# Last chunk's gelu from PSUM on ScalarE, and the last spatial pass over one token tile with its sums evacuated, added and gated

## The chip, the cores and the metric

The kernel runs on one core of one Trainium2 chip. The metric is device microseconds of one execution; lower is better. "Before" is the kernel as it was, "after" the changed one.

Engine names are those of the profile: PE is TensorE, ACT is ScalarE, DVE is VectorE, POOL is GpSimd. L12 is line 12 of the kernel that the line belongs to, so the same work has another line number in another kernel.

## The reference

Two layers, each a multi-query attention (32 heads of 16, one shared key and value head, 2048 tokens, 512 features) and a gated mixer. All inputs are bf16. Only the mixer is changed:

```python
def _B_ref(x, w_in, w_sp, b_sp, w_out):          # x [1, 2048, 512]
    z = _gelu(x @ w_in)                           # tanh form, F = 1792
    z1 = z[..., :Fh]                              # Fh = 896
    z2 = _layernorm(z[..., Fh:], axis=-1)
    g = einsum('ts,bsf->btf', w_sp, z2) + b_sp    # mixes TOKENS: [2048 x 2048]
    return (z1 * g) @ w_out

x = x + _A_ref(_layernorm(x), ...)                # layer 0
x = x + _B_ref(_layernorm(x), ...)
x = x + _A_ref(_layernorm(x), ...)                # layer 1
x = x + _B_ref(_layernorm(x), ...)
```

The product with `w_sp` needs z2 of all tokens before any output token is finished. So the end of each mixer is a serial stretch: the last tokens leave attention, pass through gelu and the norm, and only then can the last part of the sum over tokens be done. (einsum with `@` is shortened here.)

## The kernel before

The program is emitted by a small list scheduler of its own. Each operation has an engine (sometimes two to choose from), an assumed duration and a priority, and the scheduler decides the order on every engine.

The mixer works through token chunks, and the spatial product is taken in passes over token tiles of 128. Three passes run while attention still runs and leave their sums in `gp` (fp16, in SBUF); the last pass is over tiles 14 and 15:

```python
self.chunks = [512, 512, 512, 256, 128, 128]
self.passes = [(0, 8, 1), (8, 12, 2), (12, 14, 3)]   # (first tile, end, after chunk)
self.s_fin = 14                                       # last pass: tiles 14, 15
PR_SMALL = 1.0                                        # priority of the small chunks
```

The gelu of each chunk comes after its copies out of PSUM. Both z2 and z1 are copied, then both gelus run in SBUF, and the statistics of z2 wait for both:

```python
ge = sc.op("act", gl, ..., z1 + z2, -1.0, table="gelu")      # gl: gelu of z1, then of z2
...
s_ = [sc.op("dve", <bn_stats of one half of z2>, 0.53, [ge], ...) for h in range(2)]
```

The last pass adds the earlier sums inside PSUM, by a product with the identity; DVE then gates straight from PSUM (for each of 8 groups of 256 tokens):

```python
if final:
    todo.append(("g", None))                 # ident16 x gp: adds the earlier sums
todo += [("w", w) for w in ws]               # z2 x w_sp, one matmul per token tile
...
pl, (ev,) = sc.job(pieces, [dict(            # hT = PSUM * z1, 512 columns each
    fn=lambda e, b, ...: e.tensor_tensor(self.hT[:, par, f0:f0 + m, :], <PSUM>, z1r[...], ALU.mult), ...)])
```

After it come 14 matmuls of 512 columns with `w_out` for each 256 tokens, and DVE adds the residual.

The softmax here doesn't subtract the row's maximum and nothing guards it: scores larger than these inputs give would overflow.

## Time and profile before

| | before |
|---|---|
| median time, first measurement (3 runs) | 1933.82 us (1931.3 to 1937.45) |
| span of the profiled execution, mean granted clock | 1933.2 us, 0.977 |
| layer 0: last exp of attention ends / layer 1: first exp starts | 905.2 / 955.6 us |
| layer 0: last residual add, about / layer 1: first exp on DVE | 997 / 1005.5 us |
| layer 1: last exp ends, and from there to the end ("tail") | 1861.9 us, 71.3 us |

The exps of the softmax bound most of the span, so two numbers divide it well: the tail, and the time from layer 0's last exp to layer 1's last exp ("last to last", 956.7 us), which holds layer 0's transition and layer 1's attention.

Busy time by engine, from the page of before:

```profile
PE 1649.2 (85%) x17431; PEld 671.0 (35%) x17431; DVE 1777.4 (92%) x3198; ACT 1747.3 (90%) x1526; POOL 59.7 (3%) x106
```

PE, DVE and ACT are all busy on average. But the average mixes stages. The table of windows of before shows the stretch after layer 0's last exp. Its columns are: the window, its length, then busy time (and instructions) of PE, PE weight loads, DVE, ACT and POOL, then the granted clock, the share of DMA and GB/s:

```profile
925.00:945.00 20.00, 17.85 (x111) 11.95 (x112) 14.37 (x28) 0.00 (x0) 1.73 (x4) 0.83 0.18 51
945.00:965.00 20.00, 19.64 (x162) 11.61 (x160) 15.23 (x35) 11.43 (x15) 2.82 (x6) 1.00 0.27 71
...
985.00:1005.00 20.00, 17.57 (x133) 8.70 (x130) 11.85 (x23) 11.41 (x14) 1.87 (x4) 1.00 0.00 1
```

ACT, which is 90% busy over the span, has no work from 925 to 945, and the granted clock of PE is 0.83 there. The same view for the tail of layer 1:

```profile
1862.00:1882.00 20.00, 19.30 (x205) 15.42 (x203) 17.15 (x35) 6.44 (x9) 0.77 (x2) 1.00 0.34 97
1882.00:1902.00 20.00, 18.74 (x131) 12.53 (x132) 16.35 (x31) 0.00 (x0) 0.78 (x2) 1.00 0.30 90
1902.00:1922.00 20.00, 20.00 (x135) 13.01 (x133) 13.76 (x25) 0.00 (x0) 0.00 (x0) 1.00 0.45 134
```

Here PE is busy for 58 of 60 us, and ACT has nothing after 1882. PE is the limit, and the work that PE has left is the length of the tail.

The timeline of ACT at layer 1's last chunk (columns: start, duration, engine, line, operation, times; in brackets the idle time before and who ended it):

```profile
1848.69 13.24 ACT L1257 ACTIVATE Pa<-ps_all 128x1024 bf16<-128x1024 f32 x12
...
1874.53 0.54 ACT L887 ACTIVATE z2n<-ps_all 128x448 bf16<-128x448 f32 x1 [1.57 <-PE ps_all L876]
...
1876.18 1.16 ACT L913 ACTIVATE E<-ps_all 128x512 bf16<-128x512 f32 x2 [0.35 <-PE ps_all L902]
1877.36 1.28 ACT L921 ACT_TABLE_LOAD   x1
1878.66 0.95 ACT L921 ACTIVATE E<-E 128x896 bf16<-128x896 bf16 x1
1879.51 0.93 ACT L922 ACTIVATE z2n<-z2n 128x896 bf16<-128x896 bf16 x1
```

The last exps end at 1848.69 + 13.24 = 1861.93. The four copies end at 1877.34, the table load at 1878.64, both gelus at 1880.44. DVE then takes the statistics and, after a small POOL step, the normalisation:

```profile
1880.84 1.14 DVE L934 BATCH_NORM_STATS2 st_18<-z2n 128x6 f32<-128x448 bf16 x2
...
1884.09 0.51 DVE L943 TENSOR_SCALAR z2n<-z2n,mv_19,rs_21 128x896 bf16<-128x896 bf16 x1
```

So z2 is ready at 1884.60, and PE starts the last pass at 1885.25, as the timeline of PE shows:

```profile
1885.25 0.28 PE L1032 MATMUL ps_all<-gp,ident_3 128*128 128x256 f16 x1 [0.63 <-DVE gp L1050]
...
1889.30 3.19 PE L1087 MATMUL ps_all<-E 128*128 128x512 bf16 x14
```

The first line is an identity matmul. Small matmuls here have a pitch of 0.108 us, `w_out` matmuls 0.216 us (3.19 us for 14, of which the last 0.17 is drain). In layer 0 the same chain left PE idle, and then slow:

```profile
919.56 3.44 PE L1034 MATMUL ps_all<-wsT,z2n 128*128 128x256 bf16 x30
927.15 0.40 PE L1032 MATMUL ps_all<-gp,ident_3 128*128 128x256 f16 x1 [4.15 <-DVE z2n L943]
927.34 0.63 PE L1034 MATMUL ps_all<-z2n 128*128 128x256 bf16 x2
```

4.15 us idle; and the second pair of lines shows a pitch of about 0.2 us where it was 3.44 / 30 = 0.115 before the gap. The Trainium skill, "TensorE: Matmul & The Clock Gate", section Why this matters for your kernels, says that PE-idle gaps of more than about 3 us drop the matmul rate to half. This trace agrees: after 4.15 us, half pace for about 4.6 us.

The groups by form of the tail of before (busy time and mean ns of one after the first bar, idle time before them after the second):

```profile
L1032 PE MATMUL ps_all<-gp,ident_3 128*128 128x256 f16 x56 | 15.3, 273 | 0.6 <-DVE gp L1050 0.6
...
L1061 DVE TENSOR_TENSOR E<-ps_all,z1s 128x512 bf16<-128x512 f32 x24 | 15.6, 684 | 0.0
```

56 identity matmuls; and DVE's gate from PSUM takes 684 ns for 512 columns.

### The profile page before, as it was taken

How to read it: one execution, taken by the hardware profiler on the slowest of the kernel's cores; microseconds unless marked ns; L12 is line 12 of the kernel's file. 1: busy time of each engine (PE TensorE's matmuls, PEld its weight loads, DVE VectorE, ACT ScalarE, POOL GpSimd, SP SyncE). 2: the span in 40 equal slices, each digit the busy share in tenths (PEclk: the TensorE clock that was granted, in tenths of full speed). 3: DMA queues.
4: the chain of work that ended last, by engine and by line, in shares of the span. 5: the costliest groups of instructions: out<-in, count | busy, mean ns of one | idle time of the engine just before them, and what ended most of it. 6: DMA issues, size and time to landing. Idle time of an engine off the chain costs nothing.

```text
span 1933.2 us, 41389 instructions
## 1 busy us (share of the span) xinstructions
PE 1649.2 (85%) x17431; PEld 671.0 (35%) x17431; DVE 1777.4 (92%) x3198; ACT 1747.3 (90%) x1526; POOL 59.7 (3%) x106
## 2 busy tenths in 40 slices
PE   6777887787989998889987877877788999888899
PEld 3222222122234443555542222222122444335565
DVE  7999999999998898987769999989999899999976
ACT  7999999999999999997379999999999999999960
POOL 3000000000000000000000000000000000000000
PEclk9999999999999999999999999999998999989999
DMA  9700001000001000112100000010000100010123
GB/s 262 191 1 1 1 1 42 1 1 1 1 31 34 23 8 26 46 28 62 53 10 1 1 1 1 1 42 1 1 1 20 34 23 23 2 53 8 29 71 101
DMA packets 96985, 59.84 MB, mean 31 GB/s; under 512 B 39704, under 2 KB 92704, under 8 KB 96800
## 3 DMA queue, kind: packets, MB, share of 16 engines
q1 hardware_dynamic: 95216, 56.64, 10.6%
q8 instruction: 138, 2.26, 0.5%
q10 hardware_dynamic: 1584, 0.56, 0.1%
q14 instruction: 47, 0.39, 0.1%
HBM read 30.97 MB, written 17.83 MB: 25 GB/s over the span
## 4 chain that ended last, share of the span: by engine, by line
ACT 32%; PE 30%; DVE 25%; issue 12%; POOL 1%; ACTq 0%; POOLq 0%
ACT Pa L1257 29%; PE ps_all L1034 8%; PE ps_all L1540 7%; DVE E L1437 5%; PE ps_all L1333 4%; DVE Pd L1475 4%; PE ps_all L1087 3%; DVE E L1473 2%; DVE E L1464 2%; DVE E L1470 2%; DVE gp L1050 2%; PE ps_all L1523 1%; PE ps_all L748 1%; DVE E L1467 1%; ACT z2n L922 1%
## 5 line engine op out<-in xcount | busy, mean ns | idle before, releaser
L1257 ACT ACTIVATE Pa<-ps_all 128x1536 bf16<-128x1536 f32 (+1 forms) x1435 | 1640.0, 1349 | 59.6 <-PE ps_all L1540 46.0
L1540 PE MATMUL ps_all<-qs,kT 32*128 32x512 bf16 (+2 forms) x6144 | 572.8, 315 | 227.9 <-ACT Pa L1257 213.9
L1540 PEld LDWEIGHTS ps_all<-qs,kT 32*128 32x128 bf16 x6144 | 172.6, 92 | 710.1 <-ACT Pa L1257 631.0
L1437 DVE TENSOR_SCALAR E<-ps_all 128x512 int32<-128x512 f32 x510 | 347.9, 685 | 26.8 <-PE ps_all L1540 24.0
L1333 PE MATMUL ps_all<-Pa,V 128*32 128x512 bf16 (+2 forms) x5407 | 331.4, 316 | 2.0 <-DVE oT L771 1.5
L1475 DVE SCALAR_TENSOR_TENSOR Pd<-E 128x1024 uint16<-128x1024 int32 x255 | 310.2, 1217 | 0.8
L1523 PE MATMUL ps_all<-wo_r,zero 128*128 128x512 bf16 (+2 forms) x967 | 257.2, 369 | 2.2 <-DVE E L1437 1.8
L1034 PE MATMUL ps_all<-wsT,z2n 128*128 128x256 bf16 x1456 | 216.8, 276 | 4.7 <-DVE gp L1050 2.9
L1333 PE MATMUL ps_all<-Pd,V 128*32 128x512 bf16 (+2 forms) x737 | 181.0, 324 | 0.0
L1470 DVE TENSOR_TENSOR E<-E 128x1024 f16<-128x1024 f16 x255 | 174.8, 685 | 3.2
L1473 DVE TENSOR_TENSOR E<-E 128x1024 f16<-128x1024 f16 x255 | 174.4, 684 | 2.1
L1464 DVE TENSOR_SCALAR E<-E 128x1024 f16<-128x1024 uint16 x255 | 174.6, 686 | 1.1
L1034 PEld LDWEIGHTS ps_all<-wsT,z2n 128*128 128x128 bf16 x1456 | 119.5, 98 | 72.3 <-issue 36.3
L1333 PEld LDWEIGHTS ps_all<-Pa,V 128*32 128x32 bf16 x5407 | 98.7, 96 | 120.9 <-issue 99.6
L1523 PEld LDWEIGHTS ps_all<-wo_r,zero 128*128 128x128 bf16 x967 | 74.4, 100 | 122.0 <-issue 90.5
L1467 DVE TENSOR_SCALAR E<-E 128x1024 f16<-128x1024 f16 x255 | 106.9, 419 | 2.5
L1466 DVE TENSOR_SCALAR E<-E 128x1024 f16<-128x1024 f16 x255 | 107.0, 420 | 2.2
L1050 DVE TENSOR_TENSOR gp<-ps_all,gp 128x512 f16<-128x512 f32 (+1 forms) x128 | 75.3, 616 | 16.6 <-PE ps_all L1034 16.4
L748 PE MATMUL ps_all<-xnTA,wq_pad 128*128 128x512 bf16 (+2 forms) x384 | 68.8, 312 | 2.7 <-DVE E L1437 2.3
L876 PE MATMUL ps_all<-w_in_r,xnTB 128*128 128x448 bf16 x256 | 64.6, 361 | 1.3 <-DVE z2n L885 0.6
L902 PE MATMUL ps_all<-xnTB,w_in_r 128*128 128x512 bf16 (+2 forms) x336 | 63.0, 310 | 1.7 <-DVE z1s L911 1.4
L771 DVE CAST oT<-ps_all 128x512 bf16<-128x512 f32 (+2 forms) x96 | 48.7, 508 | 7.8 <-PE ps_all L1333 7.3
(79 smaller groups left out, 1168.5 us busy)
## 6 DMA issues: line engine op xcount, KB each, us to landing
wsT<-wsT_scratch SPq DMA_DIRECT2D x18, 512.0 KB, 3.9
wsT_scratch<-gp SPq DMA_DIRECT2D x16, 512.0 KB, 3.7
z1s<-z_scratch SPq DMA_DIRECT2D x16, 448.0 KB, 3.7
z_scratch<-z1s SPq DMA_DIRECT2D x6, 896.0 KB, 4.5
wsT<-wsT_scratch SPq DMA_DIRECT2D x16, 256.0 KB, 2.9
X<-in_A_x_dram SPq DMA_DIRECT2D x8, 256.0 KB, 6.4
z2n<-wsT_scratch SPq DMA_DIRECT2D x2, 1024.0 KB, 7.6
out_dram<-X SPq DMA_DIRECT2D x16, 128.0 KB, 1.7
```

Source lines behind the costliest of these rows:

```text
L1034: ins = e.matmul(o_, self.z2n[:, w[0], f * 128:(f + 1) * 128], w[1], start=st, stop=sp_)
L1050: return e.tensor_tensor(dst, src, dst, ALU.add)
L1257: return e.activation(k.Pa[:, base:base + n, :], k.b32(b0, n).rearrange("p (k q) -> p k q", k=n), ACTF.Exp, scale=SCALE)
L1333: ins = e.matmul(k.b32(k.pvb)[32 * j:32 * j + 32, 0:n], k.V[:, kt, 32 * j:32 * j + 32], b.slot[:, s * n:(s + 1) * n], tile_position=(0, 32 ...
L1437: return k.sc.op("dve", lambda e: e.tensor_scalar(k.eI[:, s, 512 * i:512 * (i + 1)], k.b32(j.bank.idx)[:, 0:512], C_LOG2, C_BIAS, op0=ALU. ...
L1464: return lambda e: e.tensor_scalar(out, a, m, None, op0=ALU.mult)
L1467: return lambda e: e.tensor_scalar(out, a, m, b, op0=ALU.mult, op1=ALU.add)
L1470: o4 = sc.op("dve", lambda e: e.tensor_tensor(q, u, w, ALU.mult), d_sb(n, 0.521e-3), [o3], pr)
L1473: o6 = sc.op("dve", lambda e: e.tensor_tensor(q, q, u, ALU.mult), d_sb(n, 0.521e-3), [o5], pr)
L1475: o7 = sc.op("dve", lambda e: e.scalar_tensor_tensor(po.bitcast(U16), I, 2.0 ** -9, q, op0=ALU.mult, op1=ALU.add), d_sb(n, 1.042e-3), [o6] ...
L1523: ins = e.matmul(k.b32(k.pvb if b is None else b.idx)[:, 0:n], k.zero[:], k.wo_r[:, 0, 0:n], start=b is not None, stop=b is not None)
L1540: ins = e.matmul(self.b32(bank)[:, s * n:(s + 1) * n], self.kT[32 * j:32 * j + 32, kt * 128:(kt + 1) * 128], self.qs[32 * j:32 * j + 32, g ...
```

## The change

Its intent: take PE work and the wait for the last gelu out of both transitions, paying with ACT and DVE time. It has five parts:

1. The last chunk's gelu is the copy out of PSUM, on ACT, and the statistics of each half of z2 wait for that half alone. The gelu table is loaded ahead by a tiny activation as soon as the layer's exps are issued, and the exp table is called back early.
2. The identity matmuls are gone. ACT (or DVE) copies the sums from PSUM to fp16, DVE adds `gp` and then multiplies by z1, both in SBUF.
3. Tile 14 moves from the last pass into the pass before it, which now runs after chunk 4.
4. The priority number of the small chunks goes from 1.0 to 0.6 (a lower number goes first).
5. A switch for merging chunks is added, but off (there is no chunk 9).

```diff
+GPL = 0                      # identity matmuls in layers below this: none
+MERGE = 9
-PR_SMALL = 1.0
+PR_SMALL = 0.6
...
-        self.passes = [(0, 8, 1), (8, 12, 2), (12, 14, 3)]
-        self.s_fin = 14
+        self.passes = [(0, 8, 1), (8, 12, 2), (12, 15, 4)]
+        self.s_fin = 15
...  # z2 (and z1 likewise): the eviction is the gelu in the last chunk
+                con = dict(fn=lambda e, b, cp=cp: e.activation(*cp(b), ACTF.Gelu_apprx_tanh), eng="act", table="gelu", ...)
-                                   [dict(fn=lambda e, b, cp=cp: e.tensor_copy(*cp(b)), ...
+                                   [con] if last else [dict(fn=lambda e, b, cp=cp: e.tensor_copy(*cp(b)), ...
...
-        ge = sc.op("act", gl, d_act(NF * n) + d_act(nt * FH), z1 + z2, -1.0, table="gelu")
+        if last:
+            gs = z2
+            pre = sc.op("act", lambda e: e.activation(self.tiny[:], self.mhalf[:], ACTF.Exp), 0.1, z1 + z2, 2.0, table="exp")
+        else:
+            gs = z1 = [sc.op("act", gl, ..., z1 + z2, -1.0, table="gelu")] * (2 * nt)
...
-                    if final:
+                    if gp_pe:                    # gp_pe = final and layer < GPL
                         todo.append(("g", None))
...
+                    pl, (ev,) = sc.job(pieces, [dict(
+                        fn=lambda e, b, cp=cp: e.tensor_copy(*cp(b)), dur=d_psum(256 * m), prio=1.1, deps=self.hT_read[par],
+                        alts=[("act", lambda e, b, cp=cp: e.activation(*cp(b), ACTF.Copy), d_act(256 * m))])], deps, pr)
+                    ad = sc.op("dve", <h16 = h16 + gp, fp16>, ..., [ev] + [self.gp_ops[(tc, f)] for f in fs], 0.9)
+                    ev = sc.op("dve", <hT = h16 * z1, bf16>, ..., [ad, zld], 0.9)
...  # after a layer's last exp has been issued
+            if not self.queue:
+                k.sc.op("act", lambda e: e.activation(k.tiny[:], k.mhalf[:], ACTF.Gelu_apprx_tanh), 0.1, [o, k.c_mh], -2.0,
+                        table="gelu")
```

(Left out: the loads of `w_sp` for the pass of three tiles, and the bookkeeping of who still reads z2.)

More of the change, by code (lines that the diff above doesn't have):

```diff
@@ L289, in job @@
             o = self.op(c.get("eng", "dve"), (lambda en, f=c["fn"]: f(en, j.bank.idx)), c["dur"],
-                        [prev] + outs[-1:] + list(c.get("deps", ())), c["prio"], job=j, alts=alts)
+                        [prev] + outs[-1:] + list(c.get("deps", ())), c["prio"], job=j, alts=alts,
+                        table=c.get("table"))
             outs.append(o)
@@ L416, in __init__ @@
         self.chunks = [512, 512, 512, 256, 128, 128]
-        self.passes = [(0, 8, 1), (8, 12, 2), (12, 14, 3)]
-        self.s_fin = 14
+        self.passes = [(0, 8, 1), (8, 12, 2), (12, 15, 4)]
+        self.s_fin = 15
+        self.merge = MERGE
         self.ring = [(0, 3), (3, 2)]
@@ L431, in __init__ @@
         self.mhalf = sb([P, 1], FP32, "mhalf")
+        self.tiny = sb([P, 1], FP32, "tiny")
         self.X = sb([P, self.NT, D], BF16, "X")
@@ L882, in cp @@
                     return self.z2n[:, t, h * 448:(h + 1) * 448], self.b32(b)[:, 0:448]
+                con = dict(fn=lambda e, b, cp=cp: e.activation(*cp(b), ACTF.Gelu_apprx_tanh), eng="act", table="gelu",
+                           dur=d_act(448), prio=pr - 1, deps=list(self.z2_read.get(t, ())))
                 pl, (ev,) = sc.job([((lambda e, b, pe=pe: pe(e, b, (0, 1))), 2 * d_mm(448)),
                                     ((lambda e, b, pe=pe: pe(e, b, (2, 3))), 2 * d_mm(448))],
-                                   [dict(fn=lambda e, b, cp=cp: e.tensor_copy(*cp(b)), dur=d_psum(448), prio=pr - 1,
+                                   [con] if last else [dict(fn=lambda e, b, cp=cp: e.tensor_copy(*cp(b)), dur=d_psum(448), prio=pr - 1,
                                          deps=list(self.z2_read.get(t, ())),
@@ L891, in mixer_chunk @@
                 self.xnTB_read.append(pl)
-        z1v = self.z1L if last else self.z1s[:].rearrange("p (f t) -> p f t", f=NF)
+        c0 = g.t0 % 512 if g.ci == self.merge + 1 else 0
+        z1v = (self.z1L if last else self.z1s[:].rearrange("p (f t) -> p f t", f=NF))[:, :, c0:c0 + n]
         z1_war = list(self.dx_s.end) if last else list(self.z1s_free)
@@ L906, in cp @@
             def cp(b, f0=f0, m=len(fs)):
-                return (z1v[:, f0:f0 + m, 0:n], self.b32(b)[:, 0:m * n].rearrange("p (f t) -> p f t", f=m))
+                return (z1v[:, f0:f0 + m, :], self.b32(b)[:, 0:m * n].rearrange("p (f t) -> p f t", f=m))
             w = max(2, 1024 // n)
+            con = dict(fn=lambda e, b, cp=cp: e.activation(*cp(b), ACTF.Gelu_apprx_tanh), eng="act", table="gelu",
+                       dur=d_act(n * len(fs)), prio=pr - 0.9, deps=z1_war)
             pl, (ev,) = sc.job([((lambda e, b, part=mm[i:i + w], pe=pe: pe(e, b, part)), len(mm[i:i + w]) * d_mm(n))
                                 for i in range(0, len(mm), w)],
-                               [dict(fn=lambda e, b, cp=cp: e.tensor_copy(*cp(b)), dur=d_psum(n * len(fs)), prio=pr - 1,
+                               [con] if last else [dict(fn=lambda e, b, cp=cp: e.tensor_copy(*cp(b)), dur=d_psum(n * len(fs)), prio=pr - 1,
                                      deps=z1_war,
@@ L917, in mixer_chunk @@
             self.xnTB_read.append(pl)
+        if g.ci == self.merge:
+            self.held = (T, z1, z2)
+            return
+        t0 = T[0]
+        if g.ci == self.merge + 1:
+            T, z1, z2 = [a + b for a, b in zip(self.held, (T, z1, z2))]
+            t0, T = T[0], T
+            z1v = self.z1s[:].rearrange("p (f t) -> p f t", f=NF)[:, :, 0:128 * len(T)]
+        nt = len(T)
         z2f = self.z2n[:].rearrange("p t f -> p (t f)")
         def gl(e):
-            e.activation(z1v[:, :, 0:n], z1v[:, :, 0:n], ACTF.Gelu_apprx_tanh)
-            return e.activation(z2f[:, T[0] * FH:(T[0] + nt) * FH], z2f[:, T[0] * FH:(T[0] + nt) * FH],
-                                ACTF.Gelu_apprx_tanh)
-        ge = sc.op("act", gl, d_act(NF * n) + d_act(nt * FH), z1 + z2, -1.0, table="gelu")
-        sp = self.dma(lambda e: e.dma_start(self.z1_dv[:, :, g.t0:g.t0 + n], z1v[:, :, 0:n]), [ge],
-                      f"z1s{g.layer}{g.ci}", n * P * NF * 2)
+            e.activation(z1v, z1v, ACTF.Gelu_apprx_tanh)
+            return e.activation(z2f[:, t0 * FH:(t0 + nt) * FH], z2f[:, t0 * FH:(t0 + nt) * FH], ACTF.Gelu_apprx_tanh)
+        if last:
+            gs = z2
+            pre = sc.op("act", lambda e: e.activation(self.tiny[:], self.mhalf[:], ACTF.Exp), 0.1, z1 + z2, 2.0, table="exp")
+        else:
+            gs = z1 = [sc.op("act", gl, d_act(NF * nt * 128) + d_act(nt * FH), z1 + z2, -1.0, table="gelu")] * (2 * nt)
+        sp = self.dma(lambda e: e.dma_start(self.z1_dv[:, :, t0 * 128:(t0 + nt) * 128], z1v), z1,
+                      f"z1s{g.layer}{g.ci}", nt * P * P * NF * 2)
         if last:
@@ L930, in mixer_chunk @@
             self.z1s_free = [sp]
-        self.z1_spill.append((g.t0, g.t0 + n, sp))
+        self.z1_spill.append((t0 * 128, (t0 + nt) * 128, sp))
         ag = []
@@ L934, in mixer_chunk @@
             s_ = [sc.op("dve", lambda e, t=t, h=h: e.bn_stats(self.st2[:, t, h, :], self.z2n[:, t, h * 448:(h + 1) * 448]),
-                        0.53, [ge], pr - 0.3) for h in range(2)]
+                        0.53, [gs[2 * (t - t0) + h]], pr - 0.3) for h in range(2)]
             ag.append(sc.op("dve", lambda e, t=t: e.bn_aggr(self.mv2[:, t, :], self.st2[:, t, :, :]), 0.13, s_, pr - 0.4))
@@ L971, in spatial @@
         nst = s1 - s0
+        early = not final and nst < 4
+        gp_pe = final and layer < GPL
         z2f = self.z2n[:].rearrange("p t f -> p (t f)")
-        if nst == 2 and not final:
+        if early:
+            slot0 = self.wsT[:, 0:8, :].rearrange("p s t -> p (s t)")
             self.wsP = []
-            self.wsP_ld = []
-            for h in range(2):
-                w_ = z2f[:, 4096:6144] if h == 0 else self.wsT[:, 0:8, :].rearrange("p s t -> p (s t)")
-                w_ = w_.rearrange("p (s t) -> p s t", s=2)
-                war = [o for t in (4, 5, 6) for o in self.z2_read[t]] if h == 0 else self.last_ws[0]
-                self.wsP.append(w_)
-                self.wsP_ld.append(self.dma(lambda e, h=h, w_=w_: e.dma_start(
-                    w_, self.ws_dv[:, s0:s1, 1024 * h:1024 * (h + 1)]), war + self.ws_st[s0:s1], f"wsp{h}", 524288, 1.0))
-            self.wsF = z2f[:, 0:4096].rearrange("p (s t) -> p s t", s=2)
+            nf = self.NT - s1
+            parts = [(0, 4, z2f[:, 2048:5120], (2, 3, 4, 5)), (4, 6, z2f[:, 5120:6656], (5, 6, 7)),
+                     (6, 8, slot0[:, 0:1536], None)]
+            if nst == 2:
+                parts = [(0, 4, z2f[:, 4096:6144], (4, 5, 6)), (4, 8, slot0, None)]
+            for (c0, c1, w_, tiles) in parts:
+                w_ = w_.rearrange("p (s t) -> p s t", s=nst)
+                war = self.last_ws[0] if tiles is None else [o for t in tiles for o in self.z2_read[t]]
+                ld = self.dma(lambda e, w_=w_, c0=c0, c1=c1: e.dma_start(w_, self.ws_dv[:, s0:s1, 256 * c0:256 * c1]),
+                              war + self.ws_st[s0:s1], f"wsp{c0}", (c1 - c0) * nst * 65536, 1.0)
+                for tc in range(c0, c1):
+                    self.wsP.append((w_[:, :, 256 * (tc - c0):256 * (tc - c0 + 1)], ld, tiles))
+            self.held_f = range(0, 3 if nf == 1 else 5)
+            self.wsF = z2f[:, 0:2048 * nf].rearrange("p (s t) -> p s t", s=nf)
             self.wsF_ld = self.dma(lambda e: e.dma_start(self.wsF, self.ws_dv[:, s1:self.NT, :]),
-                                   [o for t in range(5) for o in self.z2_read[t]] + self.ws_st[s1:], "wsf", 1048576, 1.5)
+                                   [o for t in self.held_f for o in self.z2_read[t]] + self.ws_st[s1:], "wsf", nf * 524288, 1.5)
         for tc in range(8):
@@ L990, in spatial @@
                 ws = [(s, self.wsF[:, s - s0, tc * 256:(tc + 1) * 256]) for s in range(s0, s1)]
-            elif nst == 2:
-                h, c = tc // 4, tc % 4 * 256
-                lds = [self.wsP_ld[h]]
-                ws = [(s, self.wsP[h][:, s - s0, c:c + 256]) for s in range(s0, s1)]
+                held = self.held_f
+            elif early:
+                w_, ld, held = self.wsP[tc]
+                lds = [ld]
+                ws = [(s, w_[:, s - s0, :]) for s in range(s0, s1)]
             else:
@@ L1001, in spatial @@
                 lds = [ld]
+                held = ()
                 ws = [(s, self.wsT[:, 8 * sl + s - s0, :]) for s in range(s0, s1)]
@@ L1041, in spatial @@
                     deps.append(self.l_b)
-                if final:
+                if gp_pe:
                     deps += [self.c_id16] + [self.gp_ops[(tc, f)] for f in fs]
                 m = len(fs)
-                if not final:
+                if gp_pe:
+                    pl, (ev,) = sc.job(pieces, [dict(
+                        fn=lambda e, b, par=par, f0=f0, m=m: e.tensor_tensor(
+                            self.hT[:, par, f0:f0 + m, :], self.b32(b)[:, 0:256 * m].rearrange("p (f t) -> p f t", f=m),
+                            z1r[:, par, f0:f0 + m, :], ALU.mult),
+                        dur=d_psum(256 * m), prio=0.9, deps=[zld] + self.hT_read[par])], deps, pr)
+                    hs.append(ev)
+                    ad = pl
+                elif not final:
                     def ev_fn(e, b, tc=tc, f0=f0, m=m):
@@ L1059, in spatial, with cp @@
                 else:
+                    h_ = self.hT[:, par, f0:f0 + m, :]
+                    h16 = h_.bitcast(FP16)
+                    def cp(b, h16=h16, m=m):
+                        return h16, self.b32(b)[:, 0:256 * m].rearrange("p (f t) -> p f t", f=m)
                     pl, (ev,) = sc.job(pieces, [dict(
-                        fn=lambda e, b, par=par, f0=f0, m=m: e.tensor_tensor(
-                            self.hT[:, par, f0:f0 + m, :], self.b32(b)[:, 0:256 * m].rearrange("p (f t) -> p f t", f=m),
-                            z1r[:, par, f0:f0 + m, :], ALU.mult),
-                        dur=d_psum(256 * m), prio=0.9, deps=[zld] + self.hT_read[par])], deps, pr)
+                        fn=lambda e, b, cp=cp: e.tensor_copy(*cp(b)), dur=d_psum(256 * m), prio=1.1, deps=self.hT_read[par],
+                        alts=[("act", lambda e, b, cp=cp: e.activation(*cp(b), ACTF.Copy), d_act(256 * m))])], deps, pr)
+                    ad = sc.op("dve", lambda e, h16=h16, tc=tc, f0=f0, m=m: e.tensor_tensor(
+                        h16, h16, self.gp[:, tc, f0:f0 + m, :], ALU.add), d_sb(256 * m, 0.521e-3),
+                        [ev] + [self.gp_ops[(tc, f)] for f in fs], 0.9)
+                    ev = sc.op("dve", lambda e, h_=h_, h16=h16, par=par, f0=f0, m=m: e.tensor_tensor(
+                        h_, h16, z1r[:, par, f0:f0 + m, :], ALU.mult), d_sb(256 * m, 0.521e-3), [ad, zld], 0.9)
                     hs.append(ev)
@@ L1067, in spatial @@
                     for f in fs:
-                        self.gp_read[(tc, f)] = [pl]
+                        self.gp_read[(tc, f)] = [ad]
                 users.append(pl)
@@ L1071, in spatial @@
                     self.z2_read[s].append(pl)
-                for s in range(0, 5) if final else (range(4, 7) if nst == 2 and tc < 4 else ()):
+                for s in held or ():
                     self.z2_read[s].append(pl)
-            if nst > 2:
+            if not final and not early:
                 self.last_ws[sl] = [users[-1]]
-            elif not final and tc > 3:
+            elif held is None:
                 self.last_ws[0] = [users[-1]]
```

## The prediction

> **What bounds the kernel now.** The page: ACT 90%, DVE 92%, PE 85% busy of 1933.2 us; the chain of waits is 32% ACT, 30% PE, 25% DVE. In attention, ACT runs exps back to back (1640 us), DVE taking 510 exp blocks; the change barely touches it. In the two transitions ACT idles and PE is the limit (table of windows: from 1860 to 1920 us PE is 58 of 60 us busy, ACT 8.4). Layer 1's last exp ends at 1861.9 us, so its tail lasts 71 us; layer 0's last exp ends at 905.2, layer 1's first starts at 955.6, and exps run with gaps until about 1010, the last spatial pass competing for PE.
>
> **Costs in the tail (timeline of before).** The last pass handles two token tiles plus an identity product that re-adds earlier sums: 21 matmuls of 256 columns at 0.108 us pitch, then 14 of 512 at 0.216, 5.31 us per 256 tokens, PE without gaps. Its start (1885.3) waits for the last chunk: z2 copies end 1875.8, z1 copies 1877.3, table load to 1878.7, both gelus to 1880.4, then stats queued behind other DVE work, normalise ends 1884.6. In layer 0 the same chain leaves PE idle 4.15 us, and the next 4.6 us of matmuls run at half pace (0.21 us pitch).
>
> **The change.**
> - Removes 56 identity matmuls per layer: 6.0 us PE. The emitted order shows the PE work after layer 1's last score matmul falling from 332 to 218 matmuls of 256 columns: 114 x 0.108 = 12.3 us.
> - Gelu straight from PSUM with its table loaded early: stats can start near 1876 rather than 1880.8; about 5 us off the chain.
> - Adds, per 256 tokens, 4 evacuations (58 of 64 went to ACT, about 2 us, idle there), 4 fp16 adds and 4 multiplies on DVE. A 1024-column fp16 add takes 0.685 us, pitch 0.60, so about 0.33 for 512 (estimate): 2.4 us, plus two residual adds at 0.6: 3.6 us DVE against 3.8 us PE (7x0.108 + 3.02). Balanced, so some stalls. The 2x rate for mixed fp16 and bf16 follows the Trainium skill, "VectorE: DVE Perf Modes", What auto-detection actually checks (all tensors 16-bit, unit step); no line of before shows that mix.
> - Moves tile 14 into the previous pass: 6 matmuls per evacuation, not 4.
> - Layer 0: PE order puts nearly the whole last pass ahead of layer 1's first score matmul (228 small and 109 large matmuls instead of 170+32 and 46). Summing PE costs gives 59 us plus stalls, so the first exp comes later, near 967, but then at full rate with DVE exps starting long before 1005. Before had done 69 blocks by 1010; I estimate the new kernel gets there at about 1003. DVE takes 5 blocks fewer in layer 1: 1 to 2 us back.
>
> **Sum.** Layer 1 tail 71 to about 60 us (-11); layer 0 about -6. Predicted 1917 us, 80% range 1908 to 1926. Faster by over 2% 0.04, within 2% 0.95, slower 0.01.
>
> **What would show it.** Identity matmuls gone; last exp to end 58 to 62 us; stats on z2 about 1 us after its gelu; first layer 1 exp at 962 to 972 and the last residual add of layer 0 before about 972; 512-column adds and multiplies near 0.4 us; PE over 90% busy in the tail.
>
> **What would make it wrong.** Mixed-type multiplies at half rate (0.6 us) would make DVE the limit and eat 5 to 8 us per layer; the chain evacuate-add-multiply stalling PE each 256 tokens; the delayed first exp costing more than the freed PE returns; or layer 0 gaining 10 us or more.

## More of the kernel before

`hT` has two buffers (`par = tc % 2`).

## The result, and the profile after

| | before | after |
|---|---|---|
| median, same rounds (4 runs each) | 1935.63 us (1931.3 to 1937.45) | 1915.93 us (1914.77 to 1916.67) |
| ratio, 95% interval | | 0.9901 (0.9881 to 0.9921) |
| span profiled, clock | 1933.2 us, 0.977 | 1914.8 us, 0.974 |
| layer 0's last exp ends / layer 1's first exp | 905.2 / 955.6 us | 906.7 / 968.9 us |
| last residual add of layer 0 / first exp on DVE | about 997 / 1005.5 us | 970.6 / 986.6 us |
| last to last | 956.7 us | 946.8 us |
| tail | 71.3 us | 61.3 us |

A ratio is the mean time of one kernel's fast runs over that of the other's of the same rounds, so it is not quite the ratio of the medians in the table. One per cent faster, which counts as the same at a threshold of 2%. In the two profiles the gain is 18.4 us: 10.0 in the tail, 9.9 between the last exps, less 1.5 at the start of the program.

Page and windows of after, layer 0's transition first:

```profile
PE 1634.2 (85%) x17275; PEld 655.4 (34%) x17275; DVE 1774.8 (93%) x3265; ACT 1767.6 (92%) x1573; POOL 59.3 (3%) x106
```

```profile
925.00:945.00 20.00, 19.13 (x119) 10.77 (x117) 20.00 (x53) 6.42 (x15) 0.00 (x0) 1.00 0.32 89
945.00:965.00 20.00, 17.86 (x115) 9.38 (x114) 20.00 (x57) 8.59 (x18) 1.90 (x4) 1.00 0.18 51
...
985.00:1005.00 20.00, 16.78 (x148) 5.92 (x144) 17.21 (x32) 19.88 (x19) 0.00 (x0) 1.00 0.00 1
```

PE's busy time fell by 15 us over the whole span, ACT's rose by 20. In the transition ACT now has work (the evacuations), DVE is 100% busy from 925 to 965, and PE runs at full clock; layer 1's exps start later, but from 985 on ACT is 99% busy where it was 57%.

The tail of layer 1 (windows of after, placed likewise behind its last exp at 1853.5):

```profile
1854.00:1874.00 20.00, 20.00 (x201) 16.82 (x192) 18.18 (x41) 8.72 (x17) 1.56 (x4) 1.00 0.05 13
1874.00:1894.00 20.00, 18.30 (x109) 9.92 (x106) 19.20 (x49) 5.33 (x13) 0.00 (x0) 1.00 0.48 139
1894.00:1914.00 20.00, 14.10 (x70) 6.54 (x70) 14.72 (x39) 4.36 (x10) 0.00 (x0) 1.00 0.34 104
```

In the last of these windows PE is busy only 14.1 of 20 us: over the three, 52.4 of 60, or 87%. The chain of the last chunk, on ACT and on DVE:

```profile
1853.53 1.28 ACT L1321 ACT_TABLE_LOAD   x1
...
1866.32 0.54 ACT L888 ACTIVATE z2n<-ps_all 128x448 bf16<-128x448 f32 x1 [1.58 <-PE ps_all L881]
1867.07 0.54 ACT L888 ACTIVATE z2n<-ps_all 128x448 bf16<-128x448 f32 x1 [0.21 <-PE ps_all L881]
1867.96 1.16 ACT L917 ACTIVATE E<-ps_all 128x512 bf16<-128x512 f32 x2 [0.35 <-PE ps_all L910]
```

```profile
1866.89 1.38 DVE L956 BATCH_NORM_STATS2 st_19<-z2n 128x6 f32<-128x448 bf16 x2 [0.33 <-ACT z2n L888]
...
1870.12 0.51 DVE L965 TENSOR_SCALAR z2n<-z2n,mv_20,rs_22 128x896 bf16<-128x896 bf16 x1
```

The table is loaded as the last exp ends; the first half of z2 leaves PSUM as gelu at 1866.86 and its statistics start 0.03 us later. A copy of 448 columns took 0.54 us in before, and the gelu of the same 448 columns takes 0.54 us: the function itself costs nothing in an eviction. (The Trainium skill, "ScalarE: Activation LUTs", section What ACT_TABLE_LOAD costs, says that the rate is the same for every function; this agrees.) z2 is ready at 1870.63, and PE, still busy with older work, never waits for it. In layer 0 the gap of 4.15 us is gone as well; at the same place PE works on without a pause, at a pitch near 0.115 us:

```profile
922.00 4.63 PE L1066 MATMUL ps_all<-z2n 128*128 128x256 bf16 x40
926.62 1.92 PE L1066 MATMUL ps_all<-wsT,z2n 128*128 128x256 bf16 x16
```

But further down the tail PE now waits for DVE:

```profile
1892.21 1.47 PE L1066 MATMUL ps_all<-z2n 128*128 128x256 bf16 x12
1895.84 6.22 PE L1135 MATMUL ps_all<-E 128*128 128x512 bf16 x28 [2.15 <-DVE E L1111]
1901.89 1.83 PE L1066 MATMUL ps_all<-z2n 128*128 128x256 bf16 x14
1905.85 6.22 PE L1135 MATMUL ps_all<-E 128*128 128x512 bf16 x28 [2.13 <-DVE E L1111]
```

The two waits are between the matmuls of the last pass and the `w_out` matmuls of the same tokens: PE has done the sums, and has nothing else to do until ACT has evacuated them and DVE has added and multiplied. A pair of 256-token groups takes 10.0 us here (1895.84 to 1905.85), of which PE has about 8 us of work. DVE is busy through all of both waits: the windows view of after gives it 2.84 of the 2.84 us from 1893.00 to 1895.84, and 2.25 of the 2.25 us from 1903.60 to 1905.85. The DVE groups of the tail:

```profile
L1140 DVE TENSOR_TENSOR X<-ps_all,X 128x512 bf16<-128x512 f32 x16 | 11.0, 686 | 4.8 <-PE ps_all L1135 4.7
L1108 DVE TENSOR_TENSOR E<-E,gp 128x512 f16<-128x512 f16 x24 | 9.4, 417 | 0.0
L1111 DVE TENSOR_TENSOR E<-E,z1s 128x512 bf16<-128x512 f16 x24 | 9.4, 417 | 0.0
```

Add and multiply take 417 ns each, 834 together, against 684 for the single gate from PSUM. The Trainium skill, "VectorE: DVE Perf Modes", section What auto-detection actually checks, says the double rate is taken if every tensor is 16-bit with unit step. The multiply mixes fp16 and bf16, and it takes the same 417 ns as the pure fp16 add, so the page holds here for mixed types. That this is the double rate can be estimated from two widths: the multiply takes 417 ns for 512 columns and 284 for 256, so 0.52 ns for each further column; the gate from PSUM in before took 684 and 416, so 1.05.

### The profile page after: what moved, and what is told of

Read it like the earlier page. It is cut to its first block, busy times and chain, and to the rows that moved or that the text cites. A ratio compares the mean times of both kernels' runs of the same rounds, so it can differ in the third digit from the quotient of the medians.

```text
span 1914.8 us, 41204 instructions
## 1 busy us (share of the span) xinstructions
PE 1634.2 (85%) x17275; PEld 655.4 (34%) x17275; DVE 1774.8 (93%) x3265; ACT 1767.6 (92%) x1573; POOL 59.3 (3%) x106
## 4 chain that ended last, share of the span: by engine, by line
ACT 34%; PE 28%; DVE 24%; issue 12%; POOL 1%; ACTq 0%; DVEq 0%; POOLq 0%
ACT Pa L1305 32%; PE ps_all L1591 8%; PE ps_all L1066 7%; PE ps_all L1384 5%; DVE E L1488 4%; DVE Pd L1526 3%; DVE E L1524 2%; DVE E L1521 2%; DVE E L1515 2%; PE ps_all L1574 2%; PE ps_all L1135 2%; ACT z2n L941 1%; PE ps_all L753 1%; DVE E L1518 1%; DVE gp L1090 1%
## 5 line engine op out<-in xcount | busy, mean ns | idle before, releaser
L1488 DVE TENSOR_SCALAR E<-ps_all 128x512 int32<-128x512 f32 x505 | 343.7, 684 | 28.2 <-PE ps_all L1591 25.9
L1526 DVE SCALAR_TENSOR_TENSOR Pd<-E 128x1024 uint16<-128x1024 int32 (+1 forms) x253 | 306.8, 1213 | 0.8
L1574 PE MATMUL ps_all<-wo_r,zero 128*128 128x512 bf16 (+2 forms) x923 | 250.0, 371 | 2.2 <-DVE E L1488 1.8
L1521 DVE TENSOR_TENSOR E<-E 128x1024 f16<-128x1024 f16 (+1 forms) x253 | 172.9, 683 | 3.3
L1524 DVE TENSOR_TENSOR E<-E 128x1024 f16<-128x1024 f16 (+1 forms) x253 | 172.6, 682 | 2.3
L1515 DVE TENSOR_SCALAR E<-E 128x1024 f16<-128x1024 uint16 (+1 forms) x253 | 172.7, 684 | 1.1
L1574 PEld LDWEIGHTS ps_all<-wo_r,zero 128*128 128x128 bf16 x923 | 70.2, 99 | 121.3 <-issue 91.3
L1518 DVE TENSOR_SCALAR E<-E 128x1024 f16<-128x1024 f16 (+1 forms) x253 | 105.6, 417 | 2.6
L1517 DVE TENSOR_SCALAR E<-E 128x1024 f16<-128x1024 f16 (+1 forms) x253 | 105.6, 417 | 2.2
L1107 ACT ACTIVATE E<-ps_all 128x512 f16<-128x512 f32 (+1 forms) x58 | 26.2, 563 | 43.2 <-PE ps_all L1066 43.2
```

The lines of the kernel that those rows point to most:

```text
L1488: return k.sc.op("dve", lambda e: e.tensor_scalar(k.eI[:, s, 512 * i:512 * (i + 1)], k.b32(j.bank.idx)[:, 0:512], C_LOG2, C_BIAS, op0=ALU. ...
L1515: return lambda e: e.tensor_scalar(out, a, m, None, op0=ALU.mult)
L1517: return lambda e: e.tensor_scalar(out, a, b, None, op0=ALU.add)
L1518: return lambda e: e.tensor_scalar(out, a, m, b, op0=ALU.mult, op1=ALU.add)
L1521: o4 = sc.op("dve", lambda e: e.tensor_tensor(q, u, w, ALU.mult), d_sb(n, 0.521e-3), [o3], pr)
L1524: o6 = sc.op("dve", lambda e: e.tensor_tensor(q, q, u, ALU.mult), d_sb(n, 0.521e-3), [o5], pr)
```

## The experiments

**The question.** The total came out as predicted. Was it for the reasons given? The theory: each part counts for its PE time or its chain time, so identity matmuls are worth 6.0 us per layer, the early gelu about 5 us in the tail. First rival: where the identity is removed, the chain through ACT and DVE gives the time back as PE waits. Second rival: what moves the time is the reshuffled order, above all in layer 0.

Each experiment is an edit of the changed kernel ("after"), timed in rounds with before. All gave the right result. A measure that the tables use: the tail of layer 1 is 0.108 us times the small (256-column) matmuls that PE has left after its last score matmul, plus a rest. In after that is 218 x 0.108 = 23.5 and a rest of 37.8; in before 332 x 0.108 = 35.9 and 35.4. Of the rest some 32.4 us are other work, an estimate from the trace: 112 `w_out` matmuls at 0.216 (24.2), projections and transposes of the last chunk (about 5.5), the last add and the output's transfer (about 2.7). Anything above is time in which PE waits or runs at half pace (a granted clock of 0.5, which the profiles of late_gelu, l1_late and l1_nopre have in the tail for 3.4 us each).

### id_back: identity in both layers

```diff
-GPL = 0
+GPL = 2
```

> Changed kernel with the identity matmuls put back in the last pass of both layers (sums re-added on PE, gate straight from PSUM); early gelu and the 15-tile split stay. Theory A (the gain is PE time taken out of PE-bound transitions): 56 x 0.108 = 6.0 us of PE per layer return, less the PE waits on VectorE that the evacuate-add-gate chain had caused (0.9 + 0.5 + 2.15 + 2.13 us in layer 1's tail), so 4 to 10 us slower than the changed kernel, 1920 to 1926 us. Rival R1 (the identity removal bought nothing, the vector chain ate it; the gain is the shorter gelu chain): within 2 us of the changed kernel, 1914 to 1918.

Measured: ratio 0.9940 (0.9925 to 0.9954), 1921.9 us; by ratios about 7.5 us more than after (0.0039 of 1934). Tail 67.0 us with 320 small matmuls, rest 32.4; last to last 946.3. 102 more small matmuls should have cost 11 us of tail, and the tail grew by 5.7, because the waits of PE fell from 5.66 to 1.06 us. Part of the 102 is due to the order, not to the identity: the identity itself has 56 in this layer.

### id_l0: identity in layer 0 only

```diff
-GPL = 0
+GPL = 1
```

> Identity matmuls back in layer 0 only. Theory A: about half of id_back's loss, 2 to 5 us above the changed kernel (1918 to 1921), and layer 1's tail (last exp to end) stays near 61 us while the last exp comes 2 to 5 us later. R1: 1914 to 1918. Rival R2 (layer 0's 8 us are from VectorE exps starting at 987 instead of 1005 us): if the first VectorE exp stays before 992 us, the time stays within 2 us of the changed kernel.

Measured: 0.9940 (0.9925 to 0.9956), 1922.3 us. Tail 66.1 (264 small, rest 37.6), last to last 951.1. The order of this kernel is the same as that of id_back up to layer 1's tail, so these two differ by layer 1's identity alone, and their ratios are equal: in layer 1 the identity costs nothing measurable. Both cost 7.5 us over after, although only layer 0 differs in this one, and yet the tail of layer 1 is 4.8 us longer: the edit in layer 0 left other work for it. The expectation of a tail near 61 us was missed. A warning on single profiles: with the same order up to layer 1's tail, last to last is 946.3 us in id_back's profile (clock 0.985) and 951.1 in this one (0.977), so a few us of last to last are not clear of noise.

### late_gelu: gelu after the copies again, in both layers

```diff
-                                   [con] if last else [dict(fn=...      (z2, and z1 likewise)
+                                   [dict(fn=...
-        if last:
-            gs = z2
-            pre = ...
-        else:
-            gs = z1 = [sc.op("act", gl, ...)] * (2 * nt)
+        gs = z1 = [sc.op("act", gl, ...)] * (2 * nt)
...                                      (and the early load of the gelu table taken out)
```

> Last chunk copied out of PSUM first and gelu applied afterwards in SBUF, with no early table load, as in the kernel before; the 15-tile split and the evacuate-add-gate stay. Theory A: the chain grows by about 5 us per layer, but PE has filler matmuls of the pass before for most of it, so 2 to 4 us per layer come back: 1920 to 1924 us, and PE idles 2 to 5 us waiting for the normalised z2. R1: most of the 19 us gain is lost, 1928 to 1934.

Measured: 1.0037 (1.0021 to 1.0053), 1940.3 us: 26 us over after and slower than before. Tail 74.2 (320 small, rest 39.6), last to last 960.7. Without the early gelu the other parts lose. Both expected ranges were missed. It can't be read as the price of the gelu alone: the order changed too, with 102 more small matmuls left for the tail.

### old_split: tile 14 back in the last pass

```diff
-        self.passes = [(0, 8, 1), (8, 12, 2), (12, 15, 4)]
-        self.s_fin = 15
+        self.passes = [(0, 8, 1), (8, 12, 2), (12, 14, 3)]
+        self.s_fin = 14
```

> Old split of the token tiles (12,14) and (14,16) with the evacuate-add-gate and early gelu. The number of matmuls is the same as in the changed kernel; the last pass has 14 small matmuls per 256 tokens instead of 7 (4.5 us PE against 3.8), the pass before 4 per evacuation instead of 6, so its fillers wait for VectorE (0.6 us per 0.43 us of PE). Theory A: 2 to 6 us slower than the changed kernel, 1918 to 1922 us. If the split is what mattered (rival R3): more than 8 us slower, 1924 or more.

Measured: 0.9966 (0.9947 to 0.9984), 1924.9 us: 12.6 us over after. Tail 66.7 (296 small, rest 34.7), last to last 952.3. The move of one tile seems worth more than any PE sum says. Whether that is the tile or the order needs kernels whose order stays put.

### Four kernels that keep the order until layer 1's tail

The first four all reshuffle layer 0 and with it layer 1. The next kernels change layer 1's tail alone. For l1_ident, l1_late and l1_h4 the order on PE, as emitted, is that of after up to matmul 17,069 or later of 17,275, for l1_split up to 16,814. As a check, their last to last (946.1 to 947.4 us) repeats after's 946.8.

### l1_ident: identity in layer 1 only

```diff
-        gp_pe = final and layer < GPL
+        gp_pe = final and layer == 1
```

> Changed kernel with the identity matmuls back in layer 1's last pass only; every instruction before layer 1's tail is in the same order as in the changed kernel, so only the tail can move. Tail of the changed kernel: 61.3 us = 218 x 0.108 + 32.4 of other PE work and end + 5.4 us of stalls. Theory A as predicted (6.0 us of PE work is worth 6 us): +5 to +6 us, 1921 to 1922. Theory B, formed after id_back and id_l0 differed by nothing (the identity matmuls fill PE time that the evacuate-add-gate chain otherwise leaves idle): 274 x 0.108 + 32.4 = 62.0 with no stall, so 0 to +1.5 us, 1915.5 to 1917.5.

Measured: 0.9901 (0.9885 to 0.9918), 1915.2 us: the same ratio as after. Tail 62.1 us with 274 small matmuls, 56 more, which is 6.0 us of PE; the rest fell from 37.8 to 32.5. The timeline of PE of l1_ident, where after shows waits of 2.15 and 2.13 us:

```profile
1899.16 3.19 PE L1135 MATMUL ps_all<-E 128*128 128x512 bf16 x14
...
1904.66 3.19 PE L1135 MATMUL ps_all<-E 128*128 128x512 bf16 x14 [1.22 <-DVE E L1079]
```

One wait of 1.22 us is left. So the first rival holds in layer 1: 6.0 us of matmuls were taken away, and the rest grew by 5.3 us, 4.4 of them listed waits of PE. What is left is 0.8 us of tail, and nothing that the total shows.

### l1_late: late gelu in layer 1 only

```diff
-   [con] if last else [dict(fn=...          (z2, and z1 likewise)
+   [con] if last and g.layer == 0 else [dict(fn=...
-        if last:
+        if last and g.layer == 0:
-            if not self.queue:
+            if not self.queue and nx:
```

> Changed kernel with the late gelu (copy out of PSUM, gelu in place, no early table load) in layer 1 only; the order is the same until layer 1's tail, and the tail has the same 218 small matmuls. The chain to the normalised z2 grows by about 5 us and PE has used up its fillers (the changed kernel starts the last pass 2 us after the last projection). Theory C (the earlier gelu was worth its 5 us because PE would wait): +3 to +5 us, 1919 to 1921. If fillers cover it (prediction's view that the tail is PE work): under +1.5 us.

Measured: 0.9938 (0.9925 to 0.9951), 1922.4 us: 7.2 us over after. Tail 67.1 with the same 218 small matmuls, so the 5.8 us are no matmul work of this kind. The listed waits of PE grow by 4.1 of them, and about 1.6 are half pace: 14 `w_out` matmuls near the end took 4.82 us instead of 3.19, at a granted clock of 0.66 from 1900 to 1905. The timeline of PE of l1_late:

```profile
1870.98 4.75 PE L1066 MATMUL ps_all<-wsT,z2n 128*128 128x256 bf16 x42
1876.97 1.81 PE L1066 MATMUL ps_all<-z2n 128*128 128x256 bf16 x14 [1.24 <-DVE z2n L965]
1880.91 3.20 PE L1135 MATMUL ps_all<-E 128*128 128x512 bf16 x14 [2.13 <-DVE E L1111]
...
1900.82 4.82 PE L1135 MATMUL ps_all<-E 128*128 128x512 bf16 x14 [2.13 <-DVE E L1111]
```

PE now waits 1.24 us for z2, and the waits for DVE that follow begin with the first group, as PE has no older work left to put between. The part that the theory gave as "about 5 us off the chain" is confirmed: z2 is normalised 22.7 us after layer 1's last exp, against 17.1 in after, 5.6 us later. The total lost more than the 3 to 5 us expected. That the half pace belongs to the late gelu, and is not chance of this profile, is not shown.

### l1_split: tile 14 in the last pass of layer 1 only

```diff
+        if g.layer == 1:
+            self.passes, self.s_fin = [(0, 8, 1), (8, 12, 2), (12, 14, 3)], 14
```

> Old split (12,14) and (14,16) in layer 1 only; the order is the same until shortly before layer 1's tail, and the tail happens to hold 220 small matmuls against 218: 112 of the last pass and 108 left of the pass before (against 56 and 162). Theory B: the same PE sum, and with 4.5 us PE per 256 tokens against 3.6 us VectorE fewer stalls, so -3 to +1 us, 1913 to 1917. Rival R3 (the shorter last pass itself is the gain): +4 us or more.

Measured: 0.9908 (0.9894 to 0.9921), 1915.7 us, 1.4 us over after, within the intervals. Tail 61.6, 0.3 us over after. The sum of small matmuls in the tail is 220 against 218: 112 in the last pass and 108 left over from earlier passes, against 56 and 162. A tile that is moved to an earlier pass, which is itself not done when the tail begins, is still in the tail. So old_split's 12.6 us are not this part's doing in layer 1.

### l1_h4: four buffers of hT in layer 1

The waits of 2.1 us look like a shortage of buffers: evacuation of a group into `hT` must wait for the `w_out` matmuls of the group two before. Two more buffers fit into memory that attention no longer needs (`Pd`).

```diff
-                        ... self.hT[:, par, f0:f0 + m, :] ... deps=self.hT_read[par]
+                hp = tc % 4 if layer == 1 else par
+                        ... self.hTs[hp][:, f0:f0 + m, :] ... deps=self.hT_read[hp]
```

> Changed kernel with four instead of two buffers for the gated product in layer 1's last pass (two more in the space of the VectorE exps, dead by then); the same instructions, the same order until the tail, 218 small matmuls. Theory D (the 5.4 us of stalls come from evacuations that wait for the output matmuls of two blocks back to free the buffer): -3 to -5 us, 1911 to 1913. If VectorE's own work is the limit instead: within 1 us of the changed kernel.

Measured: 0.9890 (0.9876 to 0.9904), 1912.8 us (1909.9 to 1913.2, 4 runs): about 2 us under after. Tail 59.6, rest 36.1. The timeline of PE of l1_h4:

```profile
1891.05 3.19 PE L1141 MATMUL ps_all<-E 128*128 128x512 bf16 x14
...
1900.20 3.19 PE L1141 MATMUL ps_all<-E,Pd 128*128 128x512 bf16 x14 [1.17 <-DVE Pd L1117]
1905.13 3.19 PE L1141 MATMUL ps_all<-E,Pd 128*128 128x512 bf16 x14 [1.73 <-DVE Pd L1117]
```

The waits of 2.15 and 2.13 us became 1.17 and 1.73, so in this profile part of them was the buffers. What is left may be the chain in series, or DVE's load and order: DVE is busy for 2.20 of the 2.20 us before the first of these waits ends and for 2.04 of 2.13 before the second, with adds of the pass before and residual adds too. No run took these apart. The interval overlaps with that of after. The four times lie below all of after's, but they are from other rounds, in which before was 1.8 us lower too. It is the lowest ratio measured.

### l0_late: late gelu in layer 0 only

The mirror of l1_late: layer 1 keeps the early gelu and its early table.

> Late gelu in layer 0 only. The order changes from layer 0's transition on; as emitted, layer 1's tail then holds 320 small matmuls against 218. late_gelu lost 24.3 us and l1_late 6.5, so if the two layers add: about +18 us, 1932 to 1936. Of these the tail's sum says 102 x 0.108 = 11.0 us with stalls as before, tail 71 to 73 us against 61.3; the rest, 6 to 8 us, must then show between the last exp of layer 0 and the last exp of layer 1 (946.8 us in the changed kernel). If the first part is what matters and layer 0's own chain is hidden: 1926 to 1928 with 946 to 949 us there.

Measured: 1.0018 (1.0006 to 1.0030), 1937.9 us: 22.6 us over after, more than the 18 expected. The split was missed: the tail is 68.5 (320 small, rest 33.9), shorter than expected, and last to last is 963.2, longer by 16.4 us. The order up to layer 1's tail is that of late_gelu. The early gelu matters most in layer 0. The timeline of PE of l0_late at the start of its last pass in layer 0:

```profile
927.83 2.03 PE L1066 MATMUL ps_all<-z2n 128*128 128x256 bf16 x14 [0.52 <-DVE z2n L965]
931.77 4.88 PE L1135 MATMUL ps_all<-E 128*128 128x512 bf16 x14 [1.91 <-DVE E L1111]
...
936.70 3.19 PE L1135 MATMUL ps_all<-E 128*128 128x512 bf16 x14
```

PE waited only 0.52 and 1.91 us, and yet the 14 `w_out` matmuls after it took 4.88 us where the next 14 took 3.19. (The granted clock from 925 to 935 was 0.84.) In late_gelu, same order, waits of 0.53 and 2.14 us were followed by full pace. It also happened in the tails of late_gelu (4.88 us after a wait of 2.20), l1_late and l1_nopre, but not in that of after, with waits of 2.15 and 2.13. What decides it is open; it is at most 1.7 of the 22.6 us.

### small1: old priority of the small chunks

```diff
-PR_SMALL = 0.6
+PR_SMALL = 1.0
```

> Changed kernel with the priority of the small chunks' work back at 1.0. Nothing is added or removed, only the order: 296 small matmuls are left for layer 1's tail against 218. If left-over matmuls cost their PE time: +8 us in the tail (69 to 70 us), and the attention before gives back at most 2 to 3 us for the fillers it no longer runs: 1920 to 1925. If what is left over is only a trade (done earlier or later, the same cost): within 2 us of the changed kernel.

Measured: 0.9945 (0.9930 to 0.9960), 1924.9 us: 8.5 us over after. The edit names no operation, but the expectation that none would be added or removed did not hold: the emitted program has 30 more of the dummy matmuls with zeros that the scheduler puts into gaps of PE (17,305 matmuls against 17,275), and six 512-column exps moved from ACT to DVE. Tail 67.0 (296 small, rest 35.0): 78 more small matmuls are left for the tail, 8.4 us of PE, and waits hide some. Last to last 950.7. This is the second rival shown by itself: what the scheduler makes of one priority number, order and fillers together, moves 8.5 us.

### h4: four buffers in both layers

```diff
-                hp = tc % 4 if layer == 1 else par      (against l1_h4)
+                hp = tc % 4
```

> Four buffers for the gated product in both layers. l1_h4 gained 3 us in layer 1. In layer 0 the same waits are there (0.67, 0.93 and 1.03 us of PE idle before its output matmuls), so 2 to 3 us more; but the order changes and layer 1's tail holds 248 small matmuls against 218, 3.2 us. Net 0 to -1 against l1_h4: 1911 to 1914. If below 1910 the layer 0 part is worth more than its waits.

Measured: 0.9948 (0.9935 to 0.9961), 1924.5 us, so the expectation failed: 9.1 us over after where a gain was expected. Last to last is 956.1, 9.3 us longer, the tail 64.4 (248 small). Freeing layer 0 of a buffer wait let the scheduler choose another order there, and the result is worse. Why is open; one untested rival is that the two added buffers lie in `Pd`, which layer 1's exps on DVE need soon after.

### l1_nopre: no early table load in layer 1

```diff
-            if not self.queue:
+            if not self.queue and nx:
```

> Changed kernel without the early load of the gelu table in layer 1: the load (1.28 us) then comes just before the first gelu from PSUM, on the chain; the order is otherwise the same. Theory C (the chain is not hidden): +1 to +1.5 us in the tail, 62.3 to 62.8 us; hidden: under 0.5 us. The prediction gave the early table load no separate number.

Measured: 0.9909 (0.9894 to 0.9924), 1918.0 us, 1.5 us over after and within the intervals. The expectation that the load would stand in the chain failed. The timeline of ACT of l1_nopre:

```profile
1862.41 0.60 ACT L635 ACTIVATE xnTB<-ps_all 128x512 bf16<-128x512 bf16 x1 [6.71 <-PE ps_all L626]
1863.03 1.28 ACT L888 ACT_TABLE_LOAD   x1
1864.59 0.54 ACT L888 ACTIVATE z2n<-ps_all 128x448 bf16<-128x448 f32 x1 [0.28 <-PE ps_all L881]
```

The load fell into the time in which ACT waited for PE anyway, and the gelu started as soon as PSUM was ready. The tail is 3.0 us longer (64.3). Of these, 1.0 us are listed waits (2.13, 2.13 and 2.15 us there), as the edit changed the order behind it, and about 1.6 are half pace: the last 28 `w_out` matmuls took 7.81 us where after's took 6.22. So the early table is not what the gain rests on; what is left of that part is the gelu at the eviction, with the statistics of each half waiting for that half alone. These two were not separated.

### The runs in one table

| kernel | ratio to before | last to last, us | tail, us | small matmuls in tail | rest, us | PE waits in tail, us |
|---|---|---|---|---|---|---|
| before | 1 | 956.7 | 71.3 | 332 | 35.4 | 2.63 |
| after | 0.9901 | 946.8 | 61.3 | 218 | 37.8 | 5.66 |
| id_back | 0.9940 | 946.3 | 67.0 | 320 | 32.4 | 1.06 |
| id_l0 | 0.9940 | 951.1 | 66.1 | 264 | 37.6 | 5.15 |
| late_gelu | 1.0037 | 960.7 | 74.2 | 320 | 39.6 | 5.19 |
| old_split | 0.9966 | 952.3 | 66.7 | 296 | 34.7 | 2.90 |
| l1_ident | 0.9901 | 946.9 | 62.1 | 274 | 32.5 | 1.22 |
| l1_late | 0.9938 | 947.4 | 67.1 | 218 | 43.6 | 9.80 |
| l1_split | 0.9908 | 946.1 | 61.6 | 220 | 37.8 | 4.62 |
| l1_h4 | 0.9890 | 946.2 | 59.6 | 218 | 36.1 | 3.10 |
| l0_late | 1.0018 | 963.2 | 68.5 | 320 | 33.9 | 1.73 |
| small1 | 0.9945 | 950.7 | 67.0 | 296 | 35.0 | 2.18 |
| h4 | 0.9948 | 956.1 | 64.4 | 248 | 37.6 | 3.67 |
| l1_nopre | 0.9909 | 947.7 | 64.3 | 218 | 40.8 | 6.70 |

Everything but the ratio is from the profiled execution of each. That of id_back was the fastest of its six runs, at a clock of 0.985, so its stretches look some 3 us better than its ratio. PE waits are the gaps that the timeline of PE lists from the last exp on.

## Why the prediction was right or wrong

**The total was right:** 1917 predicted, 1915.9 measured. So were the two sums: tail −11 predicted and −10.0 measured, layer 0 with what follows −6 and −9.9, the latter undersized. The sum was partly right by compensation.

**The early gelu, "about 5 us off the chain": right.** In l1_late z2 comes 5.6 us later; the tail grows by 5.8 us (4.1 of waits, about 1.6 of half pace) and the total by 7.2. It is the largest single part that was isolated. Statistics begin 0.03 us after the gelu of their half, as predicted within 1 us.

**The step that failed: "Removes 56 identity matmuls per layer: 6.0 us PE."** The PE time is real, but in layer 1 it was not on the critical path once gone: l1_ident gives the same total, and 0.8 us of tail. What the removal took from PE it gave to a chain of evacuate, add and multiply that stands between the last-pass matmuls and the `w_out` matmuls of the same tokens. The prediction had written "Balanced, so some stalls", from 3.6 us of DVE against 3.8 us of PE; it compared two sums. Its DVE sum left out other work that DVE has in the tail (adds into `gp` for the pass before, 17.1 us, and four evacuations, 2.7 us), and it left out that each group passes through the chain in series while only two `hT` buffers exist. Those stalls are chiefly two waits of about 2.1 us, in which DVE never idles. The buffers are part of them (l1_h4); how the rest divides is not shown. "PE over 90% busy in the tail" failed for the same reason: 87%, and 70% in the last 20 us.

**Why the tail still came out right.** The PE sum fell by 114 small matmuls, 12.3 us, as predicted; the rest grew by 2.4 us. The single parts, undone in layer 1 one by one, are worth 0.8 (identity), 0.3 (tile) and 5.8 us (gelu), 6.9 together and not 10.0. The rest would come from parts that hide each other's waits, and from the order that layer 0 and the priority leave behind; no run divides it. That the order can do this much is shown: small1, where only the priority number goes back, has 78 more small matmuls in the tail and 5.7 us more of it.

**Layer 0: right in its mechanism, undersized.** Predicted were a first exp of layer 1 between 962 and 972 us (968.9), residual adds over before 972 (the last begins at 970.6), and DVE exps long before 1005 (986.6). The term that was mis-sized lies behind the first exp: 69 finished exp blocks of 512 columns were put at 1003 us, 36 us after a first exp at 967; after had 70 at 999.6 us, 30.7 us after its first exp (before had 70 at 1011.1). These 3.4 us are about the 4 us that were missed. The idle 4.15 us of before and the roughly 2.3 us lost to half pace after it are absent from after's trace, but the prediction's 59 us of PE work had already left them out, and the first exp came where it said. Why the exps then ran faster than estimated is not shown.

**What stays open.** Layer 0's 9.9 us can't be divided among the parts. Undoing the tile, the priority, the identity or the gelu lengthens last to last by 5.5, 3.9, 4.3 (id_l0; in id_back's profile, with the same order, it is not longer at all) and about 14 us, which sums to far more than 9.9, and four buffers alone cost 9.3. Each of these edits reshuffles layer 0 and what is left to layer 1. The one grouping that holds, but for one kernel, is that the kernels with a late gelu in layer 0 (before, late_gelu, l0_late) have 956.7 to 963.2 us and those with an early one 946 to 952, except h4 at 956.1.

**Types and rates: right.** 417 ns for add and multiply, predicted near 0.4 us.

## What to carry to other kernels

Work taken from the busiest engine counts only if that engine does not wait instead (here 6.0 us of matmuls gave 0.8 us of tail): before crediting matmuls that an evacuate-add-multiply chain replaces, follow one group through the chain and count the buffers. Make the eviction itself do the activation where a chain waits for it, since it costs no more than a copy. Where a scheduler sets the order, undo a part only in the last stage, so that nothing before it moves; undone elsewhere, a part's cost comes mixed with that of a new order (tile 14: 12.6 us in both layers, 1.4 us in layer 1 alone). Look for stretches of half clock before reading a difference of a few us from one profile.

## What the Trainium skill lacked or had wrong

- "ScalarE: Activation LUTs", What ACT_TABLE_LOAD costs, gives about 1283 ns for the load and about 1380 ns for a drain, 2.66 us for each switch. Here the load takes the same 1.28 us, but no drain shows: in before the copy ahead of it ends at 1877.34 and the load starts at 1877.36, and the gelu after it starts at 1878.66. A switch costs about 1.3 us between back-to-back activations.
- "TensorE: Matmul & The Clock Gate", Why this matters for your kernels, gives gaps of more than about 3 us as what halves the rate. In before 4.15 us did, but in l0_late 14 `w_out` matmuls took 4.88 us and not 3.19 after gaps of only 0.52 and 1.91 us, and in late_gelu gaps of 0.53 and 2.14 us had no such effect. The same was seen in the tails of l1_late (4.82 us after a gap of 2.13) and late_gelu (4.88 after 2.20), and not in that of after (gaps of 2.15 and 2.13). So half pace was seen without a gap of 3 us, and that section has no rule that tells these cases apart.
- "VectorE: DVE Perf Modes" states its rule for tensors that are all 16-bit and does not name the mix of fp16 and bf16 in a two-source operation; here the mix runs at the double rate, 417 ns for 512 columns, like pure fp16, as the rule read literally has it.
